# Other byte addresses modulo 128 for the token, weight and h tiles of an attention and MLP kernel

## The chip, the cores and the metric

The kernel runs on one core of one Trainium2 chip. The metric is the device time of one execution, in microseconds. It was run three times; the profile is of one more execution, of which every instruction has a start and an end.

## What is computed

Linear attention, a gated MLP and a second MLP follow one another on the same 2304 tokens of 512 features, all in float32 (weights come as float64):

```python
kv = np.einsum('bhsm,bhsd->bhmd', k_p, v)            # k_p, q_p: exp features of k and q
num = np.einsum('bhsm,bhmd->bhsd', q_p, kv)
x = (num / den)                                       # -> (2304, 512)
xn = x / rms * rms_g
g = xn @ w_gate                                       # (512, 1536)
y = (silu(g) * (xn @ w_val)) @ w_out                  # (1536, 512)
h = y @ w_in                                          # (512, 2048)
out = (silu(h)) @ w2_out                              # (2048, 512)
```

## The kernel before

The 2304 tokens are cut into five blocks: four of 512 and one of 256. A block's tokens are held transposed in a tile xs0 to xs4, 128 features to a partition in four groups. Every float32 operand of the large products is held twice, as a high half rounded to float32r and a low half that is the rest, and a product is three matmuls: high by high, high by low, low by high (PASS). So a gate, value or first-MLP product of 128 output features on one block is twelve matmuls of 128x128 weights by 512 (or 256) token columns. They are written by `part` at L226.

After the attention stage (to about 218 us) `stream` runs over sweeps of two or three slices of 128 hidden features; in a sweep it goes over the five blocks, and on each block it makes the hidden slices (L226), splits them into tiles h (`split_h`: ScalarE writes the high half at L219, VectorE the low half at L220), and multiplies them by the output weights: at L280 in the gated MLP (weights stationary, h moving) and at L313 in the second MLP (h stationary, weights moving). There the pair (weights, h) changes after every three matmuls. The matmuls of one block's second product are issued between the first products of the next, so PE always has work. h tiles rotate through four buffers.

Weights are prepared while the matmuls run: a DMA on SyncE's queue brings float64 words, VectorE and GpSimd turn them into float32, `w_high` (L171) and `w_low` (L174) write the two halves into a tile w0_n or w1_n. Sweeps alternate between side 0 (six tiles, w0_0 to w0_5) and side 1 (nine tiles, w1_0 to w1_8). In a sweep of the gated MLP the first tiles are gate and value weights in turn and the last two or three are output weights; in the second MLP the first two or three are input weights and the next as many are output weights.

In the attention stage the order of the work comes from a planner (`run_order`) that holds estimated durations and numbers of buffers; it does not know addresses. The projections are the matmuls of L590, with a constant tile bd moving and tiles hl as weights.

Tiles lie one behind the other in a partition in the order in which pools and tiles are made, each rounded up to 32 bytes. The one-column constant mhalf takes 32 bytes just ahead of xs0, so that all large tiles behind it start 32 bytes past a multiple of 128. Within a tile every operand starts at a multiple of 512 bytes, so an operand's address modulo 128 is that of its tile. Three tiles, w1_0 to w1_2, lie in a pool at the other end of the memory and start at 96.

Of the kernel before, what the change touches and what calls it, by code (L numbers as in the profile page):

```python
# [8 lines left out]
F32 = mybir.dt.float32  # L9
F32R = mybir.dt.float32r  # L10
# [10 lines left out]
def kernel(  # L21
# [20 lines left out]
    P = 128  # L42
    G = 4
    KC = DM // P
    TB = 4
    scale = 1.0 / float(D) ** 0.25
    half = -0.5 * scale * scale
    eps_den = 1e-6 * M
# [9 lines left out]
    tiles += [("t", b, 0, 0) for b in range(0, B, 2)]  # L58
    blocks = [min(TB, len(tiles) - t) * P for t in range(0, len(tiles), TB)]
    NB, NE = len(blocks), 3  # L60
    tidx = {t: i for i, t in enumerate(tiles)}

    def out_rows(i):
        kind, b, hf, r = tiles[i]
        if kind == "m":
            r0 = b * S + 256 * hf
            return [(0, P, out[r0:r0 + 256, :].rearrange("(p r) d -> p r d", r=2)[:, r, :])]
        return [
            (64 * e, 64 * e + 64, out[(b + e) * S + 512:(b + e) * S + 576, :]) for e in range(2)
        ]  # L70


    const = ctx.enter_context(tc.tile_pool(name="const", bufs=1))
    big = ctx.enter_context(tc.tile_pool(name="big", bufs=1))
# [12 lines left out]
    make_identity(nc, ident)  # L87
    bd = const.tile([P, 2, 2 * P], F32R)
    g_sb = const.tile([P, DM], F32)
    mhalf = const.tile([P, 1], F32)  # L90

    xs = [big.tile([P, 2, KC, n], F32R, name=f"xs{j}") for j, n in enumerate(blocks)]
    ya = [big.tile([P, KC * blocks[j]], F32, name=f"ya{j}") for j in range(NE)]
    pools = {"w": [wa, None, None]}

# [7 lines left out]
    f = 0  # L103
# [4 lines left out]
    f = 0  # L108
# [58 lines left out]
    def w_high(job, st):  # L167
        side, slot, key, ap = job
        pool = pools["w"][2] if side and slot < W_EARLY else pools["w"][side]
        st.t = pool.tile([P, 2, KC * P], F32R, tag=f"w{side}_{slot}", name=f"w{side}_{slot}")  # L170
        nc.scalar.activation(out=st.t[:, 0, :], in_=st.m.bitcast(F32), func=AF.Copy)  # L171

    def w_low(job, st):
# [41 lines left out]
    W_PRIO, F_PRIO = 500.0, 1000.0  # L215

    def split_h(s, j):
        ht = pools["h"][0].tile([P, 2, blocks[j]], F32R, tag="h", name="h", bufs=pools["h"][1])
        nc.scalar.activation(out=ht[:, 0, :], in_=s, func=AF.Copy)  # L219
        nc.vector.tensor_tensor(out=ht[:, 1, :], in0=s, in1=ht[:, 0, :].bitcast(F32), op=ALU.subtract)  # L220
        return ht
# [16 lines left out]
    def g1_glu(f, j, hs, mid):  # L238
        prep.need((1, "g", f))
        p = ps_tile("ps_g", [P, blocks[j]])  # L240
        yield from proj(wt[1, "g", f], j, p)
        s = pools["s"][0].tile([P, blocks[j]], F32, tag="s", name="s", bufs=pools["s"][1])
        nc.scalar.activation(out=s, in_=p, func=AF.Silu)  # L243
        if blocks[j] == TB * P:
            yield from mid
        prep.need((1, "v", f))
        p = ps_tile("ps_g", [P, blocks[j]])
        yield from proj(wt[1, "v", f], j, p)
        nc.vector.tensor_tensor(out=s, in0=s, in1=p, op=ALU.mult)  # L249
        hs[f] = split_h(s, j)  # L250
        if blocks[j] < TB * P:
            yield from mid

    def g1_mlp(f, j, hs, mid, late):
        prep.need((2, "i", f))
        p = ps_tile("ps_g", [P, blocks[j]])
        yield from proj(wt[2, "i", f], j, p)
        yield from late
        s = pools["s"][0].tile([P, blocks[j]], F32, tag="s", name="s", bufs=pools["s"][1])
        nc.scalar.activation(out=s, in_=p, func=AF.Silu)  # L260
        hs[f] = split_h(s, j)
        yield from mid
# [37 lines left out]
    def g2_mlp(fs, j, hs, first, last, end):  # L300
# [7 lines left out]
        for t, d0, d1 in cuts:  # L308
# [16 lines left out]
            if last:  # L325
                for p0, p1, rows in out_rows(j * TB + t):
                    nc.sync.dma_start(out=rows[:, d0:d1], in_=o[p0:p1, t, d0:d1])
# [5 lines left out]
    def stream():  # L333
        pend = ()
        prepped = 1
        for si, (kind, fs, side) in enumerate(sweeps):
            for j in range(NB) if si < n2 else [*range(NE), *range(NB - 1, NE - 1, -1)]:
# [4 lines left out]
                for f in fs:  # L342
# [3 lines left out]
                    else:  # L346
                        short = blocks[j] < TB * P
                        keep = f == fs[0] and (end or short)
# [456 lines left out]
    def add_flip(i, key, r, rs, last):  # L805
# [3 lines left out]
        ti = tidx["m" if kind == "q" else "t", b, hf, r]  # L809
        j, o0 = divmod(ti, TB)  # L810
        o0 *= P
# [36 lines left out]
    def add_weight(job, n, gate):  # L848
        st = State()
        pr = W_PRIO + n  # L850

        def load(o):
            w_load(job, st, o.slot["raw"])

        lop = Op("ld_w", "SP", 2.0, load, gate, pr, ["raw"])
        prev = head = None
        for s in range(5):
            prev = Op(
                "w_dec", "DVE", 0.335, lambda o, s=s: w_decode(job, st, s, o.slot.get("wm")), [lop, prev], pr,
                [] if s else ["wm"], port=True,  # L860
            )
            head = head or prev
        for s in (5, 6):
            prev = Op(
                "w_add", "Pool", 1.38, lambda o, s=s: w_decode(job, st, s), [prev], pr,
                free=[(lop, "raw")] if s == 6 else [],
            )
        hi = Op("w_hi", "ACT", 0.54, lambda o: w_high(job, st), [prev], pr)
        w_done[job[2]] = Op("w_lo", "DVE", 0.61, lambda o: w_low(job, st), [hi], pr, free=[(head, "wm")], port=True)
# [98 lines left out]
    with tc.manual_schedule():  # L968
# [47 lines left out]
        n = 0  # L1016
        for j in range(NE):
            n = add_block(j, sweeps[0][1], n)
# [47 lines left out]
```

## Time and profile before

| what | value |
| --- | --- |
| time, median of three runs | 1016.66 us (1016.34 to 1016.66) |
| span of the profiled execution | 1015.2 us, 14341 instructions |
| PE busy | 1006.4 us, 99% |
| VectorE (DVE), ScalarE (ACT), GpSimd (POOL) busy | 582.5, 375.9, 282.7 us |
| DMA, mean over the span | 55 GB/s |

The profiled execution has no time of its own but its span, from the first instruction's start to the last one's end; the measured time holds what lies around it as well. PE stands for the matmuls on TensorE, PEld for its weight loads. Matmuls overlap: one starts before the recorded end of the one ahead, so a recorded duration is longer than the distance from start to start. The three views used most are the chain that ended last (what followed what, merged into groups with their count), the groups of instructions by shape, and one line's instructions in a stretch with the smallest, the median and the largest duration.

### The profile page before, as it was taken

The numbers are of one execution on the slowest core, as the hardware profiler recorded it, in microseconds if no ns is written. First come the engines' busy times: TensorE is split into PE (matmuls) and PEld (weight loads), VectorE is DVE, ScalarE is ACT, GpSimd is POOL, SyncE is SP. The second block draws the span as 40 slices with busy tenths as digits, with TensorE's granted clock in tenths as the row PEclk, the third lists the DMA queues.
The fourth block names the chain that finished last, engine by engine and source line by source line (L and its number), as shares of the span: only waits on it lengthen the run. The fifth ranks groups of instructions, "written<-read, shape, count | busy, mean of one in ns | idle before, by whom it ended". The sixth has DMA issues, their size and how long they took to land.

```text
span 1015.2 us, 14341 instructions
## 1 busy us (share of the span) xinstructions
PE 1006.4 (99%) x5423; PEld 863.5 (85%) x5423; DVE 582.5 (57%) x1289; ACT 375.9 (37%) x861; POOL 282.7 (28%) x287
## 2 busy tenths in 40 slices
PE   8999999999999999999999999999999999999998
PEld 7999998888888888888888888888888888888887
DVE  6899999727852345676332775433654544535633
ACT  6888887344221112222112334443322322322312
POOL 7656653405520013344000331321411312201300
PEclk9999999999999999999999999999999999999999
DMA  7453312202320002232000120210210210200023
GB/s 184 105 151 95 84 43 64 63 21 83 104 62 1 1 1 64 67 98 64 21 1 1 42 63 22 83 42 15 69 42 14 70 43 21 63 1 21 21 84 104
DMA packets 68725, 55.78 MB, mean 55 GB/s; under 512 B 25648, under 2 KB 62768, under 8 KB 68656
## 3 DMA queue, kind: packets, MB, share of 16 engines
q1 hardware_dynamic: 68656, 54.87, 18.4%
q8 instruction: 43, 0.70, 0.3%
q14 instruction: 26, 0.21, 0.1%
HBM read 50.14 MB, written 4.72 MB: 54 GB/s over the span
## 4 chain that ended last, share of the span: by engine, by line
PE 95%; DVE 3%; DMA 1%; SPq 0%; issue 0%; ACT 0%; POOL 0%; DVEq 0%
PE g L226 44%; PE y L313 19%; PE y L280 12%; PE b L590 5%; PE kv L673 3%; PE b L226 3%; PE b L718 3%; PE b L945 2%; PE b L704 2%; PE b L571 1%; PE b L824 1%; DVE w L174 1%; DMA va<-in_v_dram 1%; DVE m L151 0%; DVE raw L154 0%
## 5 line engine op out<-in xcount | busy, mean ns | idle before, releaser
L226 PE MATMUL g<-xs,w 128*128 128x512 f32 (+1 forms) x2256 | 472.8, 368 | 0.0
L226 PEld LDWEIGHTS g<-xs,w 128*128 128x128 f32 x2256 | 391.8, 188 | 74.1
L165 POOL TENSOR_TENSOR m<-m,raw 128x512 int32<-128x512 int32 x136 | 190.6, 1401 | 619.1 <-issue 434.9
L220 DVE TENSOR_TENSOR h<-s,h 128x512 fp32r<-128x512 f32 (+1 forms) x134 | 95.5, 713 | 187.8 <-ACT h L219 187.8
L313 PE MATMUL y<-w,h 128*128 128x512 f32 (+1 forms) x870 | 201.6, 389 | 0.0
L313 PEld LDWEIGHTS y<-w,h 128*128 128x128 f32 x870 | 162.2, 188 | 34.1
L219 ACT ACTIVATE h<-s 128x512 fp32r<-128x512 f32 (+1 forms) x134 | 78.8, 588 | 192.5 <-DVE s L249 170.5
L280 PE MATMUL y<-h,w 128*128 128x512 f32 (+1 forms) x648 | 135.6, 366 | 0.1
L280 PEld LDWEIGHTS y<-h,w 128*128 128x128 f32 x648 | 112.1, 189 | 20.5 <-DVE w L174 0.5
L260 ACT ACTIVATE s<-g 128x512 f32<-128x512 f32 (+1 forms) x80 | 44.5, 556 | 174.5 <-PE g L226 174.3
L324 DVE TENSOR_TENSOR ya<-y,ya 128x512 f32<-128x512 f32 (+1 forms) x91 | 62.3, 684 | 58.6 <-PE y L313 57.5
L249 DVE TENSOR_TENSOR s<-s,g 128x512 f32<-128x512 f32 (+1 forms) x54 | 33.9, 627 | 90.1 <-PE g L226 90.1
L291 DVE TENSOR_TENSOR ya<-y,ya 128x512 f32<-128x512 f32 (+1 forms) x80 | 50.3, 635 | 55.1 <-PE y L280 54.8
L629 ACT ACTIVATE e<-b,nb 128x128 f32<-128x128 f32 x272 | 77.5, 386 | 9.0 <-DVE nb L618 8.6
L171 ACT ACTIVATE w<-m 128x512 fp32r<-128x512 f32 x68 | 42.7, 628 | 100.8 <-POOL m L165 100.7
L590 PE MATMUL b<-bd,hl 128*128 128x256 f32 x432 | 69.3, 297 | 0.3 <-DVE hl L580 0.2
L590 PEld LDWEIGHTS b<-bd,hl 128*128 128x128 f32 x432 | 56.4, 191 | 1.8 <-DVE hl L580 0.8
L243 ACT ACTIVATE s<-g 128x512 f32<-128x512 f32 (+1 forms) x54 | 29.7, 550 | 65.9 <-PE g L226 65.7
L174 DVE TENSOR_TENSOR w<-m,w 128x512 fp32r<-128x512 f32 x68 | 51.5, 758 | 4.1 <-ACT w L171 3.8
L605 DVE TENSOR_REDUCE small<-b 128x4 f32<-128x512 f32 x72 | 50.1, 696 | 5.9 <-PE b L590 3.3
L530 POOL TENSOR_TENSOR sq<-x 128x512 f32<-128x512 f32 (+1 forms) x40 | 39.4, 987 | 33.5 <-DVE rd L744 7.3
L534 POOL TENSOR_TENSOR sq<-sq 128x256 f32<-128x256 f32 (+2 forms) x80 | 44.7, 569 | 3.3
(69 smaller groups left out, 781.7 us busy)
## 6 DMA issues: line engine op xcount, KB each, us to landing
raw<-in_moe_w_out_dram SPq DMA_DIRECT2D x28, 512.0 KB, 3.5
raw<-in_moe_w_in_dram SPq DMA_DIRECT2D x16, 512.0 KB, 3.6
raw<-in_moe_w_gate_dram SPq DMA_DIRECT2D x12, 512.0 KB, 3.5
raw<-in_moe_w_val_dram SPq DMA_DIRECT2D x12, 512.0 KB, 3.5
x<-in_k_dram SPq DMA_DIRECT2D x16, 256.0 KB, 3.4
va<-in_v_dram SPq DMA_DIRECT2D x32, 128.0 KB, 3.4
x<-in_q_dram SPq DMA_DIRECT2D x16, 256.0 KB, 3.1
out_dram<-ya SPq DMA_DIRECT2D x15, 256.0 KB, 2.0
```

The lines of the kernel that those rows point to most:

```text
L165: tt(out=mi, in0=mi, in1=(low if step == 5 else high).bitcast(I32), op=ALU.add)
L174: nc.vector.tensor_tensor(out=st.t[:, 1, :], in0=st.m.bitcast(F32), in1=st.t[:, 0, :].bitcast(F32), op=ALU.subtract)
L219: nc.scalar.activation(out=ht[:, 0, :], in_=s, func=AF.Copy)
L220: nc.vector.tensor_tensor(out=ht[:, 1, :], in0=s, in1=ht[:, 0, :].bitcast(F32), op=ALU.subtract)
L226: nc.tensor.matmul(out=ps, lhsT=w[:, a, cc * P:(cc + 1) * P], rhs=xs[j][:, c, cc, :], start=(n == 0), stop=(n == 3 * KC - 1),)
L280: nc.tensor.matmul(out=ps, lhsT=wt[1, "o", f][:, a, d * P:(d + 1) * P], rhs=hs[f][:, c, :], start=(n == 0), stop=(n == nn - 1),)
L291: nc.vector.tensor_tensor(out=y[:, d, :], in0=ps, in1=y[:, d, :], op=ALU.add)
L313: nc.tensor.matmul(out=ps, lhsT=hs[f][:, a, t * P:(t + 1) * P], rhs=wt[2, "p", f][:, c, d0:d1], start=(n == 0), stop=(n == nn - 1),)
L324: nc.vector.tensor_tensor(out=o[:, t, d0:d1], in0=ps, in1=o[:, t, d0:d1], op=ALU.add)
L590: nc.tensor.matmul(out=st.ps[:, 2 * j:2 * j + 2, :].rearrange("p h m -> p (h m)"), lhsT=st.hl[:, c, j, :], rhs=bd[:, a, :], start=(n == 0) ...
L605: nc.vector.tensor_reduce(out=st.mx, in_=st.ps, axis=AX.X, op=ALU.max)
L629: nc.scalar.activation(out=st.e[:, h, :], in_=st.ps[:, h, :], func=AF.Exp, bias=st.nb[:, h:h + 1])
```

## The change

The constant mhalf takes a whole 128 bytes, so that xs0 starts at a multiple of 128. A helper `padded` makes a tile that is some bytes longer than its content and lets the content begin some bytes in. The token tiles xs0 to xs3 are 32 bytes longer, and so are w0_0 to w0_3, w1_3, w1_4 and the four h tiles of the stream; the content of w1_3 and w1_4 begins 16 bytes in.

```diff
+    LINE, STEP = 128, 32
...
-    mhalf = const.tile([P, 1], F32)
-
-    xs = [big.tile([P, 2, KC, n], F32R, name=f"xs{j}") for j, n in enumerate(blocks)]
+    mhalf = const.tile([P, LINE // 4], F32, name="mhalf")[:, 0:1]
+
+    def padded(pool, n, shift, pad, **names):
+        t = pool.tile([P, 2 * n + pad // 4], F32R, **names)
+        return t[:, shift // 4:shift // 4 + 2 * n].rearrange("p (a n) -> p a n", a=2)
+
+    xs = [
+        padded(big, KC * n, 0, 0 if j == NB - 1 else STEP, name=f"xs{j}").rearrange("p a (c n) -> p a c n", c=KC)
+        for j, n in enumerate(blocks)
+    ]
...
-        st.t = pool.tile([P, 2, KC * P], F32R, tag=f"w{side}_{slot}", name=f"w{side}_{slot}")
+        if side == 0:
+            shift, pad = 0, STEP if slot < 4 else 0
+        else:
+            shift, pad = {3: (STEP // 2, STEP), 4: (STEP // 2, STEP)}.get(slot, (0, 0))
+        st.t = padded(pool, KC * P, shift, pad, tag=f"w{side}_{slot}", name=f"w{side}_{slot}")
...
-        ht = pools["h"][0].tile([P, 2, blocks[j]], F32R, tag="h", name="h", bufs=pools["h"][1])
+        ht = padded(pools["h"][0], blocks[j], 0, STEP, tag="h", name="h", bufs=pools["h"][1])
```

Start of each tile modulo 128, worked out from the order and the sizes of the tiles:

| tile | before | after |
| --- | --- | --- |
| xs0, xs1, xs2, xs3, xs4 | 32 each | 0, 32, 64, 96, 0 |
| w0_0 to w0_5 | 32 each | 0, 32, 64, 96, 0, 0 |
| w1_0, w1_1, w1_2 | 96 each | 96 each |
| w1_3, w1_4 | 32 each | 16, 48 |
| w1_5 to w1_8 | 32 each | 64 each |
| the four h tiles of the stream | 32 each | 0, 32, 64, 96 |
| h0, h1 of the attention stage | 32 each | 0 each |
| bd | 0 | 0 |
| hl0, hl1, hl2 | 96 each | 64 each |

The distance of a pair is the address of the moving operand less that of the weights, modulo 128.

## Rows read from the trace of the kernel before

**Rows 1.** The page: busy time by engine, and the chain by engine and line.

```profile
PE 1006.4 (99%) x5423; PEld 863.5 (85%) x5423; DVE 582.5 (57%) x1289; ACT 375.9 (37%) x861; POOL 282.7 (28%) x287
...
PE 95%; DVE 3%; DMA 1%; SPq 0%; issue 0%; ACT 0%; POOL 0%; DVEq 0%
PE g L226 44%; PE y L313 19%; PE y L280 12%; PE b L590 5%; PE kv L673 3%; PE b L226 3%; PE b L718 3%; PE b L945 2%; PE b L704 2%; PE b L571 1%; PE b L824 1%; DVE w L174 1%; DMA va<-in_v_dram 1%; DVE m L151 0%; DVE raw L154 0%
```

**Rows 2.** Span and mean granted clock of the core.

```profile
core 0: 1015.2 us, clock 1.000
```

**Rows 3.** Windows: the stretch, its length, then busy time of each engine.

```profile
25.00:100.00 75.00, 74.99 (x657) 74.04 (x657) 68.51 (x230) 64.61 (x210) 47.09 (x70) 1.00 0.46 120
...
300.00:400.00 100.00, 100.00 (x493) 84.67 (x492) 37.61 (x65) 16.64 (x31) 8.16 (x6) 1.00 0.06 16
400.00:500.00 100.00, 100.00 (x472) 83.52 (x471) 62.21 (x121) 23.47 (x41) 32.50 (x24) 1.00 0.20 64
```

**Rows 4.** The chain in order of time: start us, us, engine, tile, line, count.

```profile
618.13 8.40 PE g L226 x36
626.53 8.17 PE y L313 x36
...
692.73 8.16 PE g L226 x36
700.89 8.16 PE y L313 x36
...
1011.65 0.42 DVE ya L324
```

**Rows 5.** L226's matmuls near 692.7 and 618.1 us: duration ns smallest/median/largest.

```profile
L226 PE MATMUL g<-xs,w x36: 389/389/389, 692.6 to 700.5; 128*128 128x512 f32 x36
...
L226 PE MATMUL g<-xs,w x35: 393/398/398, 618.0 to 625.9; 128*128 128x512 f32 x35
```

**Rows 6.** Groups by shape at 287.9 and 276.7 us (busy us, mean ns), and durations.

```profile
L280 PE MATMUL y<-h,w 128*128 128x512 f32 x5 | 1.3, 393 | 0.0
...
L280 PE MATMUL y<-h,w x5: 389/393/397, 287.7 to 288.6; 128*128 128x512 f32 x5
...
L226 PE MATMUL g<-xs,w 128*128 128x512 f32 x11 | 2.7, 391 | 0.0
...
L226 PE MATMUL g<-xs,w x11: 389/389/398, 276.5 to 278.8; 128*128 128x512 f32 x11
```

**Rows 7.** Durations of 256-column matmuls: distance 0, distance 64 twice, distance 32 (L590).

```profile
L226 PE MATMUL g<-xs,w x33: 283/283/283, 346.6 to 350.5; 128*128 128x256 f32 x33
...
L226 PE MATMUL g<-xs,w x21: 280/281/281, 334.3 to 336.7; 128*128 128x256 f32 x21
...
L226 PE MATMUL g<-xs,w x19: 276/276/278, 951.7 to 953.7; 128*128 128x256 f32 x19
...
L590 PE MATMUL b<-bd,hl x432: 277/281/562, 6.4 to 157.5; 128*128 128x256 f32 x144
```

**Rows 8.** Groups by shape over the whole span: count, busy us, mean ns of one.

```profile
L226 PE MATMUL g<-xs,w 128*128 128x512 f32 x1776 | 415.7, 392 | 0.0
...
L313 PE MATMUL y<-w,h 128*128 128x512 f32 x858 | 200.1, 390 | 0.0
...
L280 PE MATMUL y<-h,w 128*128 128x512 f32 x504 | 117.6, 390 | 0.1
...
L226 PE MATMUL g<-xs,w 128*128 128x256 f32 x480 | 60.3, 282 | 0.0
...
L280 PE MATMUL y<-h,w 128*128 128x256 f32 x144 | 18.0, 282 | 0.0
```

## Prediction, made before the changed kernel was run

> **What bounds the kernel now.** The page comes first. TensorE (PE) is busy 1006.4 of 1015.2 us and the chain that ended last runs through PE for 95%, most of it at L226, L313 and L280 [rows 1]. The clock view gives a granted clock of 1.000, that is the 2.4 GHz level [rows 2]. From 300 us on, the windows show PE busy 100 of every 100 us while VectorE is at 38 to 62 and the others lower, as in the two windows kept here [rows 3]. So after the attention stage the time is a number of matmuls times the spacing from one matmul's start to the next, and the only question is what the change does to that spacing.
>
> The spacing can be read twice. In the chain, whole groups stand with their count: 36 matmuls of L226 take 8.16 us at 692.73 and 8.40 us at 618.13, the same instruction on the same shape; L313 takes 8.16 for 36 at 700.89 [rows 4]. That is 226.7 ns against 233.3 ns. In the source view the duration of one matmul is 389 ns in the first group and 393 to 398 in the second [rows 5]. So a recorded duration is the spacing plus 162 ns, and I use that to turn means into spacings: 389 is 226.7, 392 is 229.7, 390 is 227.7, and 282 for 256 columns is 120.
>
> What differs between the two groups is the address. By the table of offsets above, the slow one reads weight tiles w1_0 to w1_2, at 96 modulo 128, against token tiles at 32: distance 64. The fast one reads w0 tiles at distance 0. PE's weight loads are busy 863.5 us beside its matmuls' 1006.4 [rows 1], so the weights of the next matmul are loaded while the present one streams, and the pair that matters is a matmul's moving operand and the weights of the one behind it. Counted so over the program's order, the 3354 matmuls of 512 columns have distance 0 in 2627 cases and 64 in 727. 512 columns at 2.4 GHz are 213.3 ns, so distance 0 costs 13.3 ns over the bare stream, and distance 64 costs 20.
>
> **What the rows say of each distance.** Three things, all on the unchanged kernel.
> First, for 512 columns distance 0 is the cheapest state that lasts: 389 to the nanosecond, 36 in a row [rows 5]. Distance 64 is 6.6 ns dearer.
> Second, the spacing depends also on what came before. Five matmuls of L280 that are back at distance 0, right after a run at 64, average 393 and reach 397; eleven of L226 that follow such a run average 391, though most of them are at 389 again [rows 6]. So an unsettled matmul costs 393 less 162, 231 ns, and a run of twelve that begins with a change averages 391 less 162, 229.
> Third, 256 columns, whose bare stream is 106.7 ns, have three distances on record: 283 at distance 0 (spacing 121), 281 at 64 (119) with one stretch at 276 (114), and a median of 281 at distance 32 in the projections of L590, 277 to 562 with waits [rows 7]. None is free, and 32 is no cheaper than 64.
>
> The Trainium skill bears on this. The row: one instruction, one shape, one clock, 389 ns or 398 ns by the tile it reads [rows 5]. The page "SBUF — State Buffer", section "Who interferes with whom", gives TensorE two independent read ports, one for the moving operand and one for weights, and says that it waits on nobody. By that rule the addresses would not matter and the sum would be zero. The trace disagrees by the 6.6 ns above; the rule stays as a rival below.
> The page "TensorE: Matmul & The Clock Gate", section "Back-to-back issue gap", puts 512 columns at 215.8 ns; if every distance but 0 and 64 reached that, the sum by that page would come to some 20 us off, an estimate from that page and no end of my range.
>
> **The change part by part.** No instruction is added, removed or reordered: L220, L174, L171 and the matmuls keep their shapes, and the order of the attention stage is planned from slots, not addresses. The one-column constant grows to 128 bytes and six kinds of tile get 32 bytes; nothing is computed on the padding.
> Distances after, counted the same way: of the 3354, 780 at 0, 708 at 64, 687 and 717 at 32 and 96, 462 at odd multiples of 16 (w1_3, w1_4). Of L226's 1920, 431 are at 0, 434 at 64, 1055 (55%) elsewhere. Every run of twelve begins with another distance, and in L280 and L313 the distance changes after every three matmuls, since h tiles and their weights step on together.
>
> Let u be the spacing at the distances that no 512-column row shows. It is bounded below by 220 (the 276 ns stretch: some 7 ns over its bare stream, put on 213.3) and above by 236 (the largest duration, 398). Nearest are the two settled 512-column values, 226.7 and 233.3, since the 256-column rows put distance 32 between and not below; I take their middle, u = 230.
>
> L226, 1776 of 512 columns in the stream: now 392, so 229.7 [rows 8]. After: 0.224 x 229 (each run starts unsettled) + 0.226 x 233.3 + 0.55 x 230 = 230.5. That is +0.8 ns, +1.4 us.
> L280 and L313, 504 + 858: now 390, so 227.7 [rows 8]. After, never settled within three: 231, +3.3 ns, +4.5 us.
> 256 columns at L226 and L280, 480 + 144: now 282 [rows 8]; leaving distance 0 for the mix is worth 283 to 281 and some: -1.5 ns, -0.9 us.
> L590 goes from 32 to 64, both 281: zero; a nanosecond more on 432 would be 0.4 us, in a stage where PE is busy but VectorE is at 68.5 of 75 us and sets part of the pace [rows 3]. Matmuls of L226 and L945 in that stage, 216, stay mostly at known distances: zero, at most 0.5 us.
> VectorE, ScalarE and DMA reading from other offsets: I take zero. What hides a change is the rest of PE's 100 us; without that cover the last addition (0.42 us at 1011.65) and the loads ahead of the first work could move by tenths of a microsecond [rows 4].
>
> Sum: +1.4 + 4.5 - 0.9 = +5.0 us. The profiled span is 1015.2 us and the median of the runs 1016.66, so 1.5 us lie around it. 1015.2 + 5.0 + 1.5 = 1021.7 us, 0.5% more.
> With u = 220: L226 225.0, -8.3 us; L280 and L313 at 0.45 x 232 + 0.55 x 220 = 225.4, -3.1; 256 columns at 114 for half, -2.2: 1003 us. With u = 236: +7.3, +9.5, 0: 1033.5 us.
>
> **Rivals.** A difference under 0.2% (2 us) can't be told from none here.
> *The unseen distances are cheap.* The place is the 55% of pairs that are at neither 0 nor 64; the price is u. The time stands still at u = 227.2 (where the three terms cancel) and falls 1.7 us for each ns below. For it: the 276 ns stretch shows that half of the excess can go [rows 7], and no row excludes that a distance does it for 512 columns. Against it: distance 32 at L590 is no better than 64, and 512 columns never lasted below 389. At u = 223 it gives 1009.6 us. Chance 0.36.
> *No difference.* Either the page's rule holds and the 233 ns have another cause, or the mean over all distances happens to be today's mean, u between 226 and 228.4. Against the rule are the rows; the accident has room. 1016.7 us. Chance 0.14.
> *Dearer than forecast.* L280 and L313, changing distance every three, sit near 398 less 162 and u is at 235 too. For it: the slow group's larger value is 398 [rows 5], and matmuls after a change reach it. 1031 us. It is the upper part of the slower case, 0.12 of its 0.50.
> That the change misses part of its aim counts in all of them: w1_0 to w1_2 lie in the right-hand pool and don't move, and a quarter of the pairs stays at 0.
>
> **How the numbers follow.** Slower 0.50 (forecast 0.38 and the dear case 0.12), no difference 0.14, faster 0.36. Both signs hold much, so the range reaches from u near 220 to just under the dear case: 1004 to 1030 us; the forecast's own range is 1019 to 1027.
>
> **What will show it.** Still 5423 matmuls on PE and a granted clock of 1.000. The means by shape are the test: 393 for L226, 393 to 394 for L280 and L313, 280 for 256 columns. L226's durations should spread over several values instead of long runs of 389. If many read below 389, u was too high and the kernel is faster; if the 36-matmul groups keep 8.16 us at other distances, the address is not the cause. Wrong in another way would be a gap on PE near 212 to 232 us, where late tiles overlay those of the attention stage at shifted places.

## The result, and the profile after

The changed kernel takes 1028.04 us in the median (1027.84 to 1028.23), against 1016.66 us for the kernel before on the same chip: a ratio of 1.0113, with an interval of 1.0099 to 1.0128. It is slower by 11.4 us, where 5.0 us were forecast. Line numbers are 12 higher than before: L226 is now L238, L280 is L292, L313 is L325, L590 is L602.

The page of the kernel after shows busy time by engine, and further down the chain that ended last, by engine and by line:

```profile
PE 1018.5 (99%) x5423; PEld 862.9 (84%) x5423; DVE 583.7 (57%) x1289; ACT 375.6 (37%) x861; POOL 281.3 (27%) x287
...
PE 98%; DVE 1%; DMA 0%; issue 0%; SPq 0%; DVEq 0%
```

The counts are those of [rows 1]. PE's busy time grew by 12.1 us, that of every other engine moved by 1.4 us or less, and the span grew by 10.8. The granted clock tells whether that is the throttle:

```profile
core 0: 1026.0 us, clock 1.000
```

It is not. The windows (stretch, length, then busy time of PE, its weight loads, VectorE, ScalarE and GpSimd) say where the time lies. Before:

```profile
0.00:218.00 218.00, 212.88 (x1650) 198.71 (x1650) 179.03 (x556) 161.59 (x486) 117.07 (x169) 1.00 0.35 94
218.00:1015.00 797.00, 793.56 (x3775) 664.79 (x3773) 403.51 (x733) 214.28 (x375) 165.68 (x118) 1.00 0.14 44
```

and after:

```profile
0.00:218.00 218.00, 213.99 (x1651) 198.86 (x1652) 180.72 (x556) 161.53 (x487) 116.54 (x169) 1.00 0.35 94
218.00:1026.00 808.00, 804.49 (x3774) 664.09 (x3772) 402.96 (x733) 214.06 (x375) 164.71 (x118) 1.00 0.14 44
...
300.00:400.00 100.00, 100.00 (x485) 83.27 (x484) 36.84 (x64) 16.87 (x30) 8.21 (x6) 1.00 0.04 11
```

The attention stage ends where it did: 1651 matmuls lie ahead of 218 us, where there were 1650. The loss is behind it, in 3774 matmuls on a PE that is busy for all but the last 3.5 us: from 300 to 400 us it fits 485 of them, where it fitted 493 [rows 3]. So each takes longer, and the groups by shape (count, busy us, mean ns) say which:

```profile
L238 PE MATMUL g<-xs,w 128*128 128x512 f32 x1776 | 421.4, 395 | 0.0
L325 PE MATMUL y<-w,h 128*128 128x512 f32 x858 | 203.7, 394 | 0.0
L292 PE MATMUL y<-h,w 128*128 128x512 f32 x504 | 120.3, 395 | 0.0
...
L238 PE MATMUL g<-xs,w 128*128 128x256 f32 x480 | 59.8, 280 | 0.0
...
L292 PE MATMUL y<-h,w 128*128 128x256 f32 x144 | 17.8, 281 | 0.0
```

Against [rows 8] that is +5.7 us in L226's line, +3.6 and +2.7 us in L313's and L280's, and -0.7 us in the 256-column groups: 11.3 us, the loss but for rounding. In the chain (start us, us, engine, tile, line, count) the cheap groups are gone:

```profile
698.70 8.39 PE g L238 x36
707.09 8.36 PE y L325 x36
715.45 8.39 PE g L238 x36
723.84 8.37 PE y L325 x36
```

At this place of the program 36 matmuls took 8.16 us of either line [rows 4]; now they take 8.36 to 8.39, or 232 to 233 ns each in the mean of a group that mixes several distances. The durations of the first group (smallest, median, largest) no longer stand still at 389 as in [rows 5]:

```profile
L238 PE MATMUL g<-xs,w x36: 388/396/402, 698.5 to 706.7; 128*128 128x512 f32 x36
```

### The profile page after: what moved, and what is told of

It is laid out like the page before. It is cut to its first block, busy times and chain, and to the rows that moved or that the text cites. A ratio compares the mean times of both kernels' runs of the same rounds, so it can differ in the third digit from the quotient of the medians.

```text
span 1026.0 us, 14341 instructions
## 1 busy us (share of the span) xinstructions
PE 1018.5 (99%) x5423; PEld 862.9 (84%) x5423; DVE 583.7 (57%) x1289; ACT 375.6 (37%) x861; POOL 281.3 (27%) x287
## 4 chain that ended last, share of the span: by engine, by line
PE 98%; DVE 1%; DMA 0%; issue 0%; SPq 0%; DVEq 0%
PE g L238 46%; PE y L325 20%; PE y L292 13%; PE b L602 5%; PE b L238 3%; PE kv L685 3%; PE b L730 3%; PE b L957 2%; PE b L583 2%; PE b L716 1%; PE b L836 1%; DVE small L617 0%; DVE xt L827 0%; DMA x<-in_k_dram 0%; PE b L736 0%; DVE hl L592 0%
## 5 line engine op out<-in xcount | busy, mean ns | idle before, releaser
L238 PE MATMUL g<-xs,w 128*128 128x512 f32 (+1 forms) x2256 | 478.0, 370 | 0.0
L238 PEld LDWEIGHTS g<-xs,w 128*128 128x128 f32 x2256 | 391.5, 188 | 79.9
L325 PE MATMUL y<-w,h 128*128 128x512 f32 (+1 forms) x870 | 205.1, 392 | 0.0
L325 PEld LDWEIGHTS y<-w,h 128*128 128x128 f32 x870 | 162.3, 188 | 37.5
L231 ACT ACTIVATE h<-s 128x512 fp32r<-128x512 f32 (+1 forms) x134 | 78.8, 588 | 196.3 <-DVE s L261 173.9
L292 PE MATMUL y<-h,w 128*128 128x512 f32 (+1 forms) x648 | 138.1, 370 | 0.0
L292 PEld LDWEIGHTS y<-h,w 128*128 128x128 f32 x648 | 112.0, 188 | 22.9 <-DVE w L186 0.3
L602 PE MATMUL b<-bd,hl 128*128 128x256 f32 x432 | 69.1, 296 | 0.3 <-DVE hl L592 0.2
L602 PEld LDWEIGHTS b<-bd,hl 128*128 128x128 f32 x432 | 56.2, 191 | 2.0 <-DVE hl L592 1.0
```

The lines of the kernel that those rows point to most:

```text
L238: nc.tensor.matmul(out=ps, lhsT=w[:, a, cc * P:(cc + 1) * P], rhs=xs[j][:, c, cc, :], start=(n == 0), stop=(n == 3 * KC - 1),)
L292: nc.tensor.matmul(out=ps, lhsT=wt[1, "o", f][:, a, d * P:(d + 1) * P], rhs=hs[f][:, c, :], start=(n == 0), stop=(n == nn - 1),)
L325: nc.tensor.matmul(out=ps, lhsT=hs[f][:, a, t * P:(t + 1) * P], rhs=wt[2, "p", f][:, c, d0:d1], start=(n == 0), stop=(n == nn - 1),)
L602: nc.tensor.matmul(out=st.ps[:, 2 * j:2 * j + 2, :].rearrange("p h m -> p (h m)"), lhsT=st.hl[:, c, j, :], rhs=bd[:, a, :], start=(n == 0) ...
```

## The experiments

The distances above were counted modulo 128. Counted modulo 256, over the same pairs as in the prediction, the kernel after has another face: of the 3354 pairs of 512 columns only 185 are at 0, 595 are at 128, and 2574 at other distances; of L238's 1920 only 8 are at 0. The slow groups of before [rows 4] are then not at 64 but at 192. Theory A, formed from this: the period is 256 bytes, and of all distances only 0 lasts at 226.7 ns; nearly every other costs 229 to 234 ns. Theory B is the prediction's: the period is 128 bytes. The other letters in the expectations are rivals of single experiments. All distances below are modulo 256. The helper `padded` is the one of the change; line numbers shift by a few with each edit.

**Which period.** Two kernels push the token tiles apart and change nothing else, one by 128 bytes a tile, one by 256. The edit to the kernel before, with 128 in the first and 256 in the second:

```diff
-    xs = [big.tile([P, 2, KC, n], F32R, name=f"xs{j}") for j, n in enumerate(blocks)]
+    xs = [
+        padded(big, KC * n, 0, 0 if j == NB - 1 else 128, name=f"xs{j}").rearrange("p a (c n) -> p a c n", c=KC)
+        for j, n in enumerate(blocks)
+    ]
```

> The kernel before with xs1 to xs4 moved up by 128 bytes each against the block ahead of them; weights and h stay together. Theory A (the spacing follows the distance modulo 256, and only a distance of 0 modulo 256 settles at 226.7 ns): the blocks xs1 and xs3 now stand 128 apart from the weights, 634 matmuls of 512 columns go from 226.7 to about 232.5, the unsettled ones behind them add about 1 us, and pairs of w1_0 to w1_2 that come to 64 gain about 1.4: 1020 us. Theory B (the distance modulo 128 decides, as forecast): every pair keeps its class, 1016.7 us.

> As the run with 128, but xs1 to xs4 moved up by 256 bytes each. Theory A (modulo 256): no pair changes its class, 1016.7 us, and L226 keeps its long runs of 389 ns. Theory C (a longer period, or the mixing of distances as such, costs): 634 matmuls at 256 go to 231 or more, 1020 to 1021 us.

Measured: 1019.31 us with 128 bytes, 1.0028 (1.0018 to 1.0039) of the 1016.46 us of before; 1016.47 us with 256, 1.0000 (0.9990 to 1.0009). The chain of the first, at the weights that were all at distance 0:

```profile
694.14 8.23 PE g L233 x36
702.37 8.17 PE y L320 x36
710.54 8.33 PE g L233 x36
```

and of the second:

```profile
691.97 8.16 PE g L233 x36
700.13 8.16 PE y L320 x36
708.29 8.16 PE g L233 x36
```

Token tiles alternate between distance 0 and 128 in the first. A group of 36 spans two of them: by the order of the matmuls, 24 of the first group are at 0 and 12 at 128, and of the third 12 are at 0 and 24 at 128. At 226.7 and 233.1 ns that makes 8.24 and 8.31 us, against 8.23 and 8.33 read. L320, whose operands did not move, keeps its 8.17. A step of 256 bytes leaves every group as it was. B has no place for the 2.85 us: modulo 128 both kernels are the kernel before.

**All pairs at 0.** One tile in the other pool is made 320 bytes longer, so that w1_0 to w1_2 come to distance 0 as well.

```diff
-        st.t = pool.tile([P, 2, KC * P], F32R, tag=f"w{side}_{slot}", name=f"w{side}_{slot}")
+        pad = 320 if side and slot == 2 else 0
+        st.t = padded(pool, KC * P, 0, pad, tag=f"w{side}_{slot}", name=f"w{side}_{slot}")
```

> The kernel before with w1_0 to w1_2 moved down by 320 bytes, so that every pair of the stream has distance 0 modulo 512. Theory A and B alike (the distance is the cause): 727 matmuls go from 233.3 to 226.7, -4.8 us, fewer unsettled ones behind them, -0.7, and 256-column ones of these tiles go from 119 to 121, +0.4: 1011.5 us. Theory D (these three tiles are slow for another reason, such as their pool's place): 1016.7 us.

Measured: 1011.70 us, a ratio of 0.9953 (0.9937 to 0.9970), 4.8 us faster than before. Its groups by shape and its chain at the place that took 8.40 us in [rows 4]:

```profile
L231 PE MATMUL g<-xs,w 128*128 128x512 f32 x1776 | 411.2, 389 | 0.0
L318 PE MATMUL y<-w,h 128*128 128x512 f32 x858 | 199.3, 389 | 0.0
L285 PE MATMUL y<-h,w 128*128 128x512 f32 x504 | 117.4, 390 | 0.3 <-DVE w L179 0.3
...
L231 PE MATMUL g<-xs,w 128*128 128x256 f32 x480 | 60.7, 283 | 0.0
```

```profile
615.74 8.19 PE g L231 x36
623.92 8.16 PE y L318 x36
632.08 8.16 PE g L231 x36
```

The slow groups of before have vanished, and the means are the 389 of the settled state. So the kernel before already paid for three tiles at distance 192, and most of the gain lies in L226's line (415.7 to 411.2 us).

**One constant distance.** If distance itself costs, a distance of 128 that never changes must be slow; if only the switch from one distance to another costs, it must be as fast as 0. The kernel above, with a gap of 128 bytes between the token tiles and everything behind them, and w1_0 to w1_2 moved to match:

```diff
+    gap = wa.tile([P, 32], F32, name="gap")
+    nc.vector.memset(gap, 0.0)
...
-        pad = 320 if side and slot == 2 else 0
+        pad = 192 if side and slot == 2 else 0
```

> The run e3_all0 with all weight and h tiles moved by 128 bytes against the token tiles: L226 has one distance, 128 modulo 256, throughout, and L280 and L313 keep 0. Theory A (the distance itself costs, settled or not): 1776 matmuls of 512 columns at 232.5 to 233.4 instead of 226.7, +10.5 to +12 us on 1011.7: 1022 to 1024 us. Theory B (modulo 128): 1011.7. Theory F (the cost is that of changing the distance, not of the distance): 1012 to 1013 us.

Measured: 1023.44 us against 1016.50, a ratio of 1.0068 (1.0053 to 1.0083), and 11.7 us more than the kernel it was made from. Chain and groups by shape:

```profile
697.25 8.39 PE g L233 x36
705.64 8.17 PE y L320 x36
713.81 8.39 PE g L233 x36
722.21 8.17 PE y L320 x36
```

```profile
L233 PE MATMUL g<-xs,w 128*128 128x512 f32 x1776 | 422.1, 395 | 0.0
L320 PE MATMUL y<-w,h 128*128 128x512 f32 x858 | 199.8, 390 | 0.0
```

The pairs of L233 at 128 cost 8.39 / 36 = 233.1 ns in the mean, 36 in a row; L320, whose two operands moved together, keeps 8.17. A distance that never changes thus costs 6.4 ns without any switch, and moving both operands costs nothing. For the prediction this is the plainest contradiction: modulo 128 this kernel has all its pairs at 0.

**The address alone.** Only mhalf is made 128 bytes long; every large tile but w1_0 to w1_2 moves by 96 bytes, and the pairs with those three go from distance 192 to 32.

```diff
-    mhalf = const.tile([P, 1], F32)
+    mhalf = const.tile([P, 32], F32, name="mhalf")[:, 0:1]
```

> The kernel before with only the constant made 128 bytes long, so that everything behind it moves by 96 bytes and the large tiles start at multiples of 128. Theory A: w1_0 to w1_2 go from 192 to 32 modulo 256, both near 233.3, all else keeps distance 0: 1016.7 us within 0.5. Theory H (the start of a tile modulo 128 matters by itself, for PE, VectorE or the loads): another time by more than 2 us.

Measured: 1015.59 us, 0.9990 (0.9980 to 0.9999). L226's group stays, at 415.4 us against 415.7, and the pairs now at 32 take the 8.40 us that they took at 192:

```profile
L226 PE MATMUL g<-xs,w 128*128 128x512 f32 x1776 | 415.4, 391 | 0.0
```

```profile
617.35 8.40 PE g L226 x36
```

No effect over the 2 us that the rival asked for. The 0.9 us is a little more than was allowed for. In the profiled executions the streams behind the attention stage differ by 0.6 us, spread over several groups; where it comes from stays open.

**The h tiles alone.** Each h tile gets 32 bytes; w1_3 is shifted so that no other distance changes.

```diff
+        shift = 384 if side and slot == 3 else 0
+        st.t = padded(pool, KC * P, shift, shift, tag=f"w{side}_{slot}", name=f"w{side}_{slot}")
...
+        ht = padded(pools["h"][0], blocks[j], 0, 32, tag="h", name="h", bufs=pools["h"][1])
```

> The kernel before with the four h tiles of the stream 32 bytes apart, and w1_3 kept at its old class. Theory A: in L280 and L313 the distance changes every three matmuls and nothing settles; some 1360 matmuls go from 227.7 to 231 to 233 and the first matmuls of L226 behind them are unsettled: +5 to +8 us, 1022 to 1025. Theory E (only the long runs of L226 feel the distance): 1016.7 us.

Measured: 1022.26 us, 1.0057 (1.0042 to 1.0072), 5.8 us over before. Groups by shape:

```profile
L231 PE MATMUL g<-xs,w 128*128 128x512 f32 x1776 | 416.1, 392 | 0.0
L318 PE MATMUL y<-w,h 128*128 128x512 f32 x858 | 203.7, 394 | 0.0
L285 PE MATMUL y<-h,w 128*128 128x512 f32 x504 | 120.0, 395 | 0.0
```

The second products have the means they have after the whole change, 394 and 395, and L231 keeps its 392. This one edit makes nearly the whole loss of those two lines.

It also shows that a switch of distance has a price of its own. Sorted by the addresses of their own two operands, 357 of these second products are still at distance 0, in runs of three between others. From one start to the next they take 231.2 ns in the mean, and not the 226.7 of a long run, and so do the 275 of them that are at 0 from the next matmul's weights as well. The 1003 at other distances take 232.4.

**The change without one of its parts.** The changed kernel, once without the steps and shifts of the weight tiles (`shift, pad = 0, 0`), once without the steps of the h tiles. In the second, w1_3 and the tiles behind it are moved up by the 128 bytes that the h tiles give back, so that no other pair changes. The edit of the second:

```diff
-            shift, pad = {3: (STEP // 2, STEP), 4: (STEP // 2, STEP)}.get(slot, (0, 0))
+            shift, pad = {3: (STEP // 2 + LINE, STEP + LINE), 4: (STEP // 2, STEP)}.get(slot, (0, 0))
...
-        ht = padded(pools["h"][0], blocks[j], 0, STEP, tag="h", name="h", bufs=pools["h"][1])
+        ht = padded(pools["h"][0], blocks[j], 0, 0, tag="h", name="h", bufs=pools["h"][1])
```

> The changed kernel with the steps and shifts of the weight tiles undone; xs and h keep their 32-byte steps. Theory A with the spacings read so far for each distance modulo 256 (226.7 at 0, 229.3 at 64, 233 to 234.4 elsewhere): three pairs in four still stand off 0 modulo 256 and those that come to 0 are few, so undoing this part gives nothing back: 1028 to 1030 us. Rival (each part adds its own share): clearly under 1028.

> The changed kernel with the steps of the h tiles undone, the weight tiles kept at their classes modulo 128. Theory A by the same spacings: 1026 to 1028 us, since the h tiles now stand together but not at 0 from their weights. Rival (each part adds its own share, h alone was worth 5.8 us): 1022 us.

Measured: 1028.62 us without the weight steps, 1.0116 (1.0101 to 1.0131), and 1025.73 without the h steps, 1.0089 (1.0072 to 1.0106), the latter just under what was expected. The groups by shape, without the weight steps:

```profile
L235 PE MATMUL g<-xs,w 128*128 128x512 f32 x1776 | 421.0, 394 | 0.0
L322 PE MATMUL y<-w,h 128*128 128x512 f32 x858 | 203.8, 394 | 0.0
```

and without the h steps:

```profile
L238 PE MATMUL g<-xs,w 128*128 128x512 f32 x1776 | 421.2, 395 | 0.0
L325 PE MATMUL y<-w,h 128*128 128x512 f32 x858 | 203.1, 393 | 0.0
L292 PE MATMUL y<-h,w 128*128 128x512 f32 x504 | 118.4, 391 | 0.0
```

The parts don't add. The h steps alone cost 5.8 us, but taking them out of the change gives back 2.3; the weight steps give back nothing. That fits one cheap distance: one step is enough to take a pair off 0, and a second one on the same pair finds little left to spoil.

**Small distances.** Is there a cheap distance finer than 32 bytes? The kernel with all pairs at 0, with ten kinds of weight tiles (the expectation says eleven) shifted by 4 to 48 bytes. With the lengthened tiles ahead of them, L234's pairs come to distances from 144 to 252, and most of those of L321 to 20, 40, 76, 80 and 112:

```diff
+        shift, pad = (
+            {0: (28, 32), 1: (20, 32), 2: (48, 256), 3: (20, 32), 4: (8, 32), 5: (16, 192)}
+            if side else {0: (4, 32), 1: (-24 + 32, 32), 2: (12, 32), 3: (16, 160)}
+        ).get(slot, (0, 0))
```

> The run e3_all0 with eleven weight tiles moved by small and by odd amounts, so that L226's pairs stand at other distances modulo 256: 252, 216, 176, 144 on side 0 and 228, 204, 144, 236, 216, 176 on side 1 (to within what the slots give). It is a map, one value for each tile's runs of twelve. Theory A: no distance settles below 226.7 and the kernel is at 1017 to 1023 us. Rival G (a finer distance is cheaper than 0): groups of L226 that settle below a duration of 389 ns.

Measured: 1026.81 us, 1.0101 (1.0081 to 1.0121), above the expected 1017 to 1023. Its chain and groups by shape:

```profile
621.40 8.39 PE g L234 x36
629.79 8.45 PE y L321 x36
```

```profile
L234 PE MATMUL g<-xs,w 128*128 128x512 f32 x1776 | 421.6, 394 | 0.0
L321 PE MATMUL y<-w,h 128*128 128x512 f32 x858 | 204.6, 395 | 0.0
L288 PE MATMUL y<-h,w 128*128 128x512 f32 x504 | 117.7, 390 | 0.0
```

The finer distances are no cheaper; L321's group at 8.45 / 36 = 234.7 ns, which mixes distances 20, 40 and 80, is dearer than any of one distance shown here. L288, whose pairs were left at 0, keeps 390. A was right in kind, but I had priced these distances too low again.

**A version that beats both.** For 256 columns distance 0 is not the best [rows 7]. The kernel with all pairs at 0, with xs4, the block of 256 tokens, 192 bytes further on:

```diff
+        padded(big, KC * n, 192 * (j == NB - 1), 256 * (j == NB - 1), name=f"xs{j}").rearrange("p a (c n) -> p a c n", c=KC)
```

> The run e3_all0 with the 256-token block xs4 alone moved to distance 192 modulo 256. Theory A with the values read so far for 256 columns (283 ns at 0, 276 to 281 at 192): 480 matmuls gain 2 to 3 ns, up to 6 where they settle at 276: 1009.5 to 1011 us. Rival (256 columns are bound by something else): 1011.7 us.

Measured: 1010.45 us, 0.9941 (0.9926 to 0.9956), the fastest kernel here: 6.1 us under the kernel before and 17.6 under the changed one. Groups by shape:

```profile
L234 PE MATMUL g<-xs,w 128*128 128x512 f32 x1776 | 411.0, 389 | 0.0
...
L234 PE MATMUL g<-xs,w 128*128 128x256 f32 x480 | 59.8, 281 | 0.0
```

The 480 matmuls of 256 columns went from 60.7 to 59.8 us, which is most of the 1.25 us by which the time fell.

## Why the prediction was right in direction and wrong in size

**Right.** The bound and the mechanism: PE alone sets the time, the clock stays at 1.000, no instruction was added, and the distance between moving operand and weights sets the spacing, though with another period. The 1028.04 us lies within the range of 1004 to 1030 and above the forecast's own 1019 to 1027. That the sign came out right owes something to luck: below u = 227.2 the same sum forecasts a faster kernel, and u was a choice. The 256-column groups came to 280 and 281 against a forecast of 280 (-0.7 us against -0.9). The durations spread over several values. No gap opened near the end of the attention stage, and VectorE and ScalarE, taken at zero, are within 1.2 us of their old busy time. That L590's line would stay at zero held too: its 432 matmuls are busy 69.1 us, against 69.3. L226's 144 matmuls in the attention stage grew from 35.4 to 36.1 us, a little over the 0.5 us allowed, without making that stage longer.

**The step that failed** is L226's term, "0.224 x 229 + 0.226 x 233.3 + 0.55 x 230 = 230.5". It measured 395 less 162, that is 233 (232.6 by the starts in the trace), and +5.7 us in place of +1.4. It rests on a period of 128 bytes that nothing had shown, and two of its factors were too low. "0.224 x 229" took 431 pairs as cheap because they are at 0 modulo 128; 8 of them are at 0 modulo 256, the others at 128, which costs 233.1 (one constant distance, above). At 233 for 229 that is 0.224 x 4 = 0.9 ns, or 1.6 us. "u = 230" was the middle between 226.7 and 233.3; the distances that could not be seen cost about 233, the upper of the two, which is 0.55 x 3 = 1.65 ns, or 2.9 us. With both corrected the term is 233.1. The half nanosecond left is the factor in the middle: most of the pairs priced at 233.3 stand at 64 and not at 192, and by the starts the 264 of them in the stream take 230.2 ns. The first products of the kernel before showed only the distances 0 and 192, and from two points I had taken a period that neither of them proves; the middle between them was a choice, and 233.3 was in the bounds.

**The second term**, "231, +3.3 ns, +4.5 us" for L280 and L313, measured 232 to 233 and +6.3 us. It too was mis-sized and not misplaced: I had priced all of those pairs as unsettled ones on their way back to 226.7. The kernel with only the h steps shows that 231 is the price of the ones at distance 0, 231.2 ns; the larger part stands at other distances and pays 232.4. The two misses, 4.3 and 1.8 us, make up the difference between +5.0 and the +10.8 of the span; small terms of both signs cancel beside them.

**The rivals.** "The unseen distances are cheap" falls: no group of 512 columns lasted under 226.7 ns in any kernel here. "No difference" falls with the constant distance: 11.7 us between two kernels that differ by a gap of 128 bytes in the layout and one short VectorE instruction. The Trainium skill's rule in "SBUF — State Buffer", section "Who interferes with whom", by which TensorE's two read ports are independent and TensorE waits on nobody, does not carry over to the time here: 226.7 ns at distance 0 and 233.1 at 128. Why the distance counts no run shows. "Dearer than forecast", 1031 us, came nearest; its u of 235 and the forecast's 230 lie on either side of the 233 measured.

**Left open.** Which weights make the pair, the matmul's own or those loaded for the next, was not told apart: within a run of matmuls both stand at the same distance. The 0.9 us of the moved base was not traced.

## What to carry to other kernels

In a stretch where PE never pauses, read the spacing per tile from groups of the chain with their counts before touching a layout: two values for one shape that sort by the tile read point to an address effect and what it is worth, and the cheapest group shows the goal. Skewing addresses to spread operands apart is no gain in itself: here the best layout for 512 columns is the opposite, every operand pair at the same address modulo 256, and one stray pool of three tiles cost the tuned kernel 4.8 us. Find the period with two small steps (128 and 256 bytes) before counting which pairs a change leaves alone.

## What the runs showed of the hardware

With 512 columns in float32r and a weight load for every matmul, the spacing has one cheap distance among those tried: 0 modulo 256, at 226.7 ns (8.16 us for 36). Distances 128, 192 and 32 cost 233.1 to 233.3 (8.39 and 8.40 us for 36), a mix of 20, 40 and 80 up to 234.7. Distance 64 lies between: with the token tiles 128 bytes apart, the pairs with w1_0 to w1_2 are at 192 and 64, 24 to 12 in the first of these groups and 12 to 24 in the second:

```profile
619.83 8.36 PE g L233 x36
...
636.37 8.29 PE g L233 x36
```

By the starts in that trace, L233's matmuls at 64 take 229.4 ns in the mean of 333. The absolute address does nothing over the 0.9 us of the moved base. With 256 columns the order is another: durations of 283 ns at distance 0, 281 in the mean with xs4 at 192. The latter is not shown to be the best: in the kernel with small distances, 55 matmuls at 204 have starts 113.3 ns apart, against 117.8 with xs4 at 192 and 119.7 at 0.

A recorded duration tells the spacing of a single matmul, and not only of a group. In the kernel with the constant distance of 128, 3108 of the stream's 3139 matmuls of 512 columns last 160 to 163 ns longer than the time from their start to that of the next. So the spread of durations at one distance is real, here in the group at 697.25 us:

```profile
L233 PE MATMUL g<-xs,w x36: 387/394/398, 697.1 to 705.2; 128*128 128x512 f32 x36
```

The starts alternate: at 128 they lie mostly 229 and 237 to 238 ns apart in turn, and 233.1 is the mean of the two; in the kernel before, at distance 192, the turns are 231 and 236 ns. At 0 a long run keeps 226 to 227.
